# Turning 12 of 16 token tiles by DMA transposes of 16-bit planes instead of by TensorE

## The chip, the cores and the metric

The kernel runs on one core of a Trainium2 chip. The metric is the device time of one execution in microseconds, the median of several runs. The engines are called PE (TensorE, matmuls), DVE (VectorE), ACT (ScalarE), POOL (GpSimd) and SP (SyncE, which here only issues DMAs). The engines run beside one another and wait for each other by semaphores; on each engine the instructions run in a fixed order.

## The reference

The input is 2048 tokens of 512 numbers. They are normalised, and the normalised tokens go into a linear attention with a softmax feature map and into a mixture of 8 experts with two experts per token; both results are added to the input. Cut to what matters here:

```
xn = layernorm(x)                                  # x: 1 x 2048 x 512
q, k, v = split(xn @ wqkv)                         # 32 heads of 16
pq, pk = q @ w_phi, k @ w_phi                      # per head
phi(p) = concat(softmax(p), softmax(-p))
kv = phi(pk).T @ v                                 # per head, summed over all tokens
a = (phi(pq) @ kv) / (phi(pq) @ sum(phi(pk)))  @ wo
gates = softmax(xn @ wg); the two largest, scaled to sum 1
b = sum over the two of gate * (gelu(xn @ w1[e]) @ w2[e])
out = x + a + b
```

## The kernel before, in words

The 2048 tokens are 16 tiles of 128 tokens (one token per partition), and 4 chunks of 4 tiles. A tile `t` goes through these steps, each a function of the kernel:

- `load_x` loads x by DMA (two tiles share a buffer); `stats(t)` takes mean and variance on DVE; `rstds(t0, n)` makes 1/sqrt for n tiles at once: a square root on ACT and a reciprocal on DVE. `ln_stats` is stats and rstds of four tiles together. `norm(t)` normalises on DVE and stores the rows to `xn_rows` by a DMA of SP; the experts gather tokens from there later.
- `transp(t)` turns the tile, so that features lie on partitions, as a matmul's operand must: `turn` lets PE transpose four blocks of 128 x 128 into PSUM (L326); ACT then casts the result to a rounded high part `xTh` (L341), and DVE subtracts that to get the low part `xTl` (L342). Products are made of the three terms high·high, low·high and high·low, so every projection has 12 matmuls (4 blocks of features, 3 terms).
- `proj_v(t)`, `proj_k(t)` make values and key features of a tile on PE; `proj_q(c, b)` makes a quarter of the features of the queries of chunk c. ACT copies each result out of PSUM (`pV` L361, `pK` L429 and, for the gates, L430, `pQ` L479).
- The key features' softmax: `k_sub(t)` (four DVE instructions, L439 to L442), `k_exp(t)` (ACT's Exp, L449), `k_norm(t)` (three DVE instructions, L454 to L456). `kv(t)` then adds phi(k)ᵀv of the tile on PE, 64 small matmuls per tile (L501).

These steps are called one by one in an order written out by hand. The order of the calls is the order on each engine: PE, ACT, DVE and SP are queues that each run their instructions in that order, and an instruction whose input is not ready holds all behind it on its engine. PE starts with the folded weights and with tiles 0 to 3, then come the chunks of tiles 4 to 7, 8 to 11 and 12 to 15. In this stage kv of tiles 0 to 7 is made. Behind `k_norm(7)` DVE starts the routing (the first instruction is the maximum over the gates, L535), while PE goes on with the remaining queries, values and kv. After the routing come gathers and the experts.

Sqrt and Exp need different tables on ACT; a change between them loads one (the rows named ACT_TABLE_LOAD).

Buffers in SBUF are handed out from fixed pools by `slot` and given back by `free`; with `keep=True` the slot comes from the pool `keptN`.

Of the kernel before, what the change touches and what calls it, by code (L numbers as in the profile page):

```python
# [39 lines left out]
def kernel(  # L40
# [11 lines left out]
    nc = tc.nc  # L52
    P = 128
# [71 lines left out]
    def slot(shape, dt=F32, name="s", keep=False):  # L125

        n = 1
        for d in shape[1:]:
            n *= d
        words = n // 2 if dt == F16 else n  # L130
        kind = "R" if dt == F32R else "N"
        sizes = range(0 if words <= SIZES[0] else 1, 2)
        count[0] += 1
        k = choose_slot(kind, sizes, keep)
        _, b = spare[k].pop(0)
        if b is None:
# [172 lines left out]
    xn = {}  # L309

    def norm(t):
        n = slot([P, D], name="xn")
        nc.vector.tensor_scalar(n, xt[t // 2][:, t % 2, :], mv[:, t, 0:1], rstd[:, t:t + 1],
                                op0=ALU.subtract, op1=ALU.mult)
        nc.sync.dma_start(xs[t * 512:(t + 1) * 512, :].rearrange("(p a) f -> p (a f)", a=4), n)
        xn[t] = n
        if t % 2:
            free(xt.pop(t // 2))

    turned = {}  # L320

    def turn(t):
        a = bank("pT")
        turned[t] = a, bank("pT") if t < 4 else a
        for k in range(KD):
            nc.tensor.transpose(turned[t][k // 2][:, k * P:(k + 1) * P], xn[t][:, k * P:(k + 1) * P], ident)  # L326
        free(xn.pop(t))

    def transp(t):
        c, j = divmod(t, TPC)  # L330
        if j == 0:
            xTh[c] = [slot([P, 2, 512], F32R, name="xTh", keep=c == 1) for _ in range(2)]
            xTl[c] = [slot([P, 2, 512], F32R, name="xTl", keep=c == 1) for _ in range(2)]
        if t not in turned:
            turn(t)
        ps = turned.pop(t)
        for h in range(2):
            dh = xTh[c][h][:, :, j * P:(j + 1) * P]
            dl = xTl[c][h][:, :, j * P:(j + 1) * P]
            src = ps[h][:, h * 256:(h + 1) * 256].rearrange("p (k n) -> p k n", k=2)  # L340
            nc.scalar.copy(dh, src)  # L341
            nc.vector.tensor_sub(dl, src, f32(dh))  # L342
        free(*ps[:2 if t < 4 else 1])


    vt = {}
# [6 lines left out]
    def proj_v(t, then=None):  # L353
        c, j = divmod(t, TPC)
        if t % 2 == 0:
            vt[t // 2] = slot([P, 2, 32, 18], name="v", keep=t >= 8)
            nc.gpsimd.memset(vt[t // 2][:, :, :, 16:18], 1.0)
        ps = bank("pV")
        mm3(ps, [xcol(c, k, j) + (wvh[k // 2][:, k % 2, :], wvl[k // 2][:, k % 2, :]) for k in range(KD)],
            then)  # L360
        nc.scalar.copy(vt[t // 2][:, t % 2, :, 0:16], ps.rearrange("p (b j) -> p b j", j=16))  # L361
        free(ps)
        if t == NT - 1:
            free(*wvh, *wvl)
# [378 lines left out]
    def ln_stats(t0):  # L743
        for t in range(t0, t0 + TPC):
            stats(t)
        rstds(t0, TPC)
# [101 lines left out]
    proj_k(3)  # L848
    for t in range(8, 12):
        load_x(t)  # L850
    ln_stats(4)
    for t in range(4, 8):
        norm(t)
    k_sub(0)
    proj_v(0)
    proj_v(1)
    k_sub(1)
    proj_v(2)
    proj_v(3)
    for t in range(4, 8):  # L860
        transp(t)
    for t in range(8, 12):
        stats(t)
    proj_v(4)
    proj_v(5)
    rstds(8, TPC)
    for t in range(8, 12):
        norm(t)
    k_exp(0, 1)
    k_sub(2)  # L870
    proj_v(6)
    k_sub(3)
    for t in range(12, 16):
        load_x(t)
    proj_v(7)
    k_norm(0)
    proj_k(4)
    k_exp(2, 3)
    proj_k(5)
    k_norm(1)  # L880
    for t in range(8, 12):
        transp(t)
    k_norm(2)
    proj_k(6)
    k_norm(3)
    k_sub(4)
    proj_k(7)
    k_sub(5)

    for b in range(3):  # L890
        proj_q(0, b)
    kv(0)
    kv(1)
    k_exp(4, 5)
    k_norm(4)
    ln_stats(12)
    for t in range(12, 16):
        norm(t)
    k_sub(6)
    proj_k(8)  # L900
    kv(2)
    kv(3)
    proj_k(9)
    proj_k(10)
    proj_k(11)
    proj_q(0, 3)
    for t in range(12, 16):
        transp(t)
    k_norm(5)
    k_sub(7)  # L910
    k_exp(6, 7)
    k_norm(6)
    proj_k(12)
    proj_k(13)
    proj_k(14)
    kv(4)
# [796 lines left out]
```

## Time and profile before

| | |
|---|---|
| median of 3 runs | 859.4 us (858.75 to 859.9) |
| profiled execution | 858.56 us |
| its span | 856.8 us |
| granted PE clock, mean | 1.0 |
| PE busy | 851.3 us |
| DVE busy | 663.9 us |
| ACT busy | 438.7 us |
| POOL busy | 184.4 us |

The span runs from the first to the last instruction of the profiled execution; its own time is 1.76 us longer. In the rows of the timeline, the first number is the start in us from the span's start, the second the length; then come engine, line of the kernel, operation, result <- inputs with their shapes, and how many instructions the row stands for. In brackets stands the idle time of the engine just before it and what ended that. Matmuls overlap, so a row is longer than the pace at which the next one starts.

### The profile page before, as it was taken

To read this page: it belongs to the slowest core of one execution; us is meant where nothing else is said; L and a number is where in the kernel's file an instruction comes from. 1 tells how busy PE (TensorE), PEld (TensorE's weight loads), DVE (VectorE), ACT (ScalarE), POOL (GpSimd) and SP (SyncE) were. 2 spreads that over 40 slices of the span, in tenths; PEclk is the share of its full clock that TensorE was granted. 3 is DMA by queue.
4 is the path that set the end of the run, shared out by engine and by line. 5 is a ranking of instruction groups with operands and counts; after the bars stand their busy time and mean duration, and the time that the engine had idled before them with its cause. 6 is when DMAs were issued, how large, how long until landed. Compare 5 with 4: busy or idle time off the path is not lost.

```text
span 856.8 us, 15997 instructions
## 1 busy us (share of the span) xinstructions
PE 851.3 (99%) x5889; PEld 767.9 (90%) x5889; DVE 663.9 (77%) x1098; ACT 438.7 (51%) x721; POOL 184.4 (22%) x251
## 2 busy tenths in 40 slices
PE   9999999999999999999999999999999999999998
PEld 8888888899999999999999999998787888888886
DVE  6889899887783478878887877987798989846952
ACT  4453522743834364566456665465675566434541
POOL 5000002010004112511241142115511522340011
PEclk9999999999999999999999999999999999999999
DMA  8220106573317441843364346533752736539733
GB/s 298 99 99 2 50 8 191 167 231 101 123 50 221 143 133 37 253 133 113 97 200 151 111 138 159 176 110 123 229 178 87 232 115 205 175 135 384 258 115 100
DMA packets 123575, 126.99 MB, mean 148 GB/s; under 512 B 12518, under 2 KB 87782, under 8 KB 123488
## 3 DMA queue, kind: packets, MB, share of 16 engines
q1 hardware_dynamic: 115408, 106.10, 38.6%
q0 software_dynamic: 7264, 19.36, 7.0%
q8 instruction: 48, 0.79, 0.4%
q10 hardware_dynamic: 816, 0.43, 0.2%
q14 instruction: 39, 0.32, 0.1%
HBM read 98.62 MB, written 27.25 MB: 147 GB/s over the span
## 4 chain that ended last, share of the span: by engine, by line
PE 99%; DMA 0%; DVE 0%; issue 0%
PE pH L174 12%; PE pH L175 12%; PE pH L176 12%; PE pY L1296 9%; PE pY L1334 6%; PE pY L1335 6%; PE pY L1340 6%; PE pY L1266 4%; PE pY L1336 2%; PE pY L1337 2%; PE pY L1342 2%; PE pV L174 2%; PE pK L174 2%; PE pQ L474 2%; PE pV L176 2%; PE pO L176 2%
## 5 line engine op out<-in xcount | busy, mean ns | idle before, releaser
L1220 ACT ACTIVATE gl<-pH 128x276 f32<-128x276 f32 (+6 forms) x182 | 78.1, 436 | 252.6 <-PE pH L176 237.4
L1225 DVE TENSOR_TENSOR h<-gl,h 128x480 fp32r<-128x480 f32 (+6 forms) x112 | 77.8, 695 | 96.5 <-ACT h L1222 76.8
L1233 POOL DMA_INDIRECT y_rows<-keptN,pidx x83 | 90.6, 1091 | 253.3 <-ACT gl L1220 210.1
L176 PE MATMUL pH<-keptR,ws 128*128 128x258 f32 (+3 forms) x276 | 82.8, 300 | 0.0
L174 PE MATMUL pH<-keptR,ws 128*128 128x270 f32 (+3 forms) x240 | 72.5, 302 | 0.0
L175 PE MATMUL pH<-keptR,ws 128*128 128x270 f32 (+3 forms) x240 | 72.4, 301 | 0.0
L1222 ACT CAST h<-gl 128x480 fp32r<-128x480 f32 (+6 forms) x112 | 70.1, 626 | 3.6
L175 PE MATMUL pH<-xgl,ws 128*128 128x260 f32 (+3 forms) x204 | 64.6, 317 | 0.0
L174 PE MATMUL pH<-xgh,ws 128*128 128x260 f32 (+3 forms) x204 | 64.6, 317 | 0.0
L1335 PE MATMUL pY<-h,ws 128*128 128x388 f32 (+4 forms) x180 | 62.4, 347 | 0.0
L276 ACT CAST ws<-keptN 128x1024 fp32r<-128x1024 f32 x55 | 57.5, 1046 | 6.9 <-PE pY L1266 6.9
L176 PE MATMUL pH<-xgh,ws 128*128 128x272 f32 (+3 forms) x188 | 59.2, 315 | 0.0
L276 ACT CAST keptR<-keptN 128x1024 fp32r<-128x1024 f32 (+4 forms) x75 | 50.6, 705 | 16.4 <-remote 4.4
L1334 PE MATMUL pY<-h,ws 128*128 128x416 f32 (+4 forms) x168 | 58.5, 348 | 0.0
L1296 PE MATMUL pY<-h,ws 128*128 128x480 f32 x228 | 56.3, 381 | 0.0
L971 POOL DMA_INDIRECT keptN<-xn_rows,tidx x30 | 34.3, 1145 | 97.0 <-DVE vv L675 46.9
L279 DVE TENSOR_TENSOR ws<-keptN,ws 128x1024 fp32r<-128x1024 f32 x36 | 43.6, 1211 | 13.9 <-ACT ws L276 13.6
L176 PEld LDWEIGHTS pH<-keptR,ws 128*128 128x128 f32 x276 | 52.1, 189 | 1.3
L1296 PEld LDWEIGHTS pY<-h,ws 128*128 128x128 f32 x228 | 42.3, 188 | 10.8 <-issue 2.9
L175 PEld LDWEIGHTS pH<-keptR,ws 128*128 128x128 f32 x240 | 45.3, 189 | 2.2
L176 PE MATMUL pH<-xgh,keptR 128*128 128x272 f32 (+3 forms) x148 | 47.1, 318 | 0.0
L174 PEld LDWEIGHTS pH<-keptR,ws 128*128 128x128 f32 x240 | 45.1, 188 | 1.2
(339 smaller groups left out, 2397.1 us busy)
## 6 DMA issues: line engine op xcount, KB each, us to landing
keptN<-in_B_w_dram SPq DMA_DIRECT2D x172, 256.0 KB
wr<-in_B_w_dram SPq DMA_DIRECT2D x52, 256.0 KB
keptN<-y_rows SPq DMA_DIRECT2D x16, 512.0 KB
x_slots<-keptN SPq DMA_DIRECT2D x25, 256.0 KB
keptN<-in_A_x_dram SPq DMA_DIRECT2D x16, 256.0 KB
xn_rows<-keptN SPq DMA_DIRECT2D x16, 256.0 KB
keptN<-x_slots SPq DMA_DIRECT2D x32, 128.0 KB
keptN<-in_A_x_dram SPq DMA_DIRECT2D x8, 512.0 KB
```

Source lines behind the costliest of these rows:

```text
L174: nc.tensor.matmul(ps, lh, rh, start=(i == 0), stop=False)
L175: nc.tensor.matmul(ps, lh, rl, start=False, stop=False)
L176: nc.tensor.matmul(ps, ll, rh, start=False, stop=(i == n - 1))
L276: nc.scalar.copy(dst_h, src)
L1220: step[:] = [nc.scalar.activation(g[:, c:c + m], ps[:, :m], AF.Gelu_apprx_tanh)]
L1222: nc.scalar.copy(h[:, 0:full], g)
L1225: nc.vector.tensor_sub(h[:, xw:], g, f32(h[:, 0:full]))
L1233: i = nc.gpsimd.indirect_dma_start(out=to, out_offset=bass.IndirectOffsetOnAxis(ap=rows, axis=0), in_=y, in_offset=None)
L1296: nc.tensor.matmul(ps[i][:, 0:w], ws[z][:, D + i * P:D + i * P + P], h[:, low * xw:low * xw + w], start=st and k == 0, stop=last and k == ...
L1334: nc.tensor.matmul(ps[i][:, 0:w - P], vh, h[:, P:w], start=st, stop=False, skip_group_check=True)
L1335: nc.tensor.matmul(ps[i][:, 0:m], vl, h[:, P:cap], start=False, stop=False, skip_group_check=True)
L1340: nc.tensor.matmul(ps[i][:, 0:m], v[0][:, i * P:(i + 1) * P], h[:, gw + P:], start=False, stop=sp_, skip_group_check=True)
```

## The change

Tiles 4 to 15 are no longer turned by PE. A float32 number is two 16-bit numbers. For each of these tiles:

- `norm` writes the tile to the first half of a buffer of twice the size, and no longer stores it; the store is a step of its own, `keep_rows`, called later.
- `to_planes(t)`: an ACT copy of 128 x 1024 16-bit numbers (L331 of the new kernel) puts all the upper and all the lower halves of the numbers into two planes; then one DMA transpose, issued by SP (L335), turns these 8 blocks of 128 x 128 16-bit numbers into a buffer `pl`, which two tiles share.
- `to_words(t)`: an ACT copy of the same size (L340) joins the planes to float32 numbers again.
- `transp(t)` casts and subtracts as before (L365, L366), from SBUF instead of PSUM.

48 of the 64 transposes of L326 go, and with them 12 PSUM banks; 24 ACT copies and 12 DMA transposes come. `rows_apart(t)` is `keep_rows`, `to_words` and `transp`.

The order of the calls changes too. The first chunk's queries, `proj_q(0, 0)` to `proj_q(0, 3)`, stand ahead of `proj_v(4)`; before, three of them stood ahead of `kv(0)` and the last ahead of the turning of tiles 12 to 15. The loads, statistics and norms of tiles 12 to 15 come earlier; `ln_stats(12)` is taken apart into stats and `rstds(12, TPC)`. `k_norm`, `proj_k` and `k_sub` are moved among them.

```diff
     def norm(t):
-        n = slot([P, D], name="xn")
+        both = slot([P, 2, D], name="xn")
+        n = both[:, 0, :]
         nc.vector.tensor_scalar(n, xt[t // 2][:, t % 2, :], mv[:, t, 0:1], rstd[:, t:t + 1],
                                 op0=ALU.subtract, op1=ALU.mult)
-        nc.sync.dma_start(xs[t * 512:(t + 1) * 512, :].rearrange("(p a) f -> p (a f)", a=4), n)
-        xn[t] = n
+        xn[t] = both
+        if t < 4:
+            keep_rows(t)
...
+    def keep_rows(t):
+        nc.sync.dma_start(xs[t * 512:(t + 1) * 512, :].rearrange("(p a) f -> p (a f)", a=4), xn[t][:, 0, :])
+
+    def to_planes(t):
+
+        a = xn[t].bitcast(U16)
+        nc.scalar.copy(a[:, 1, :].rearrange("p (h c) -> p h c", h=2),
+                       a[:, 0, :].rearrange("p (c h) -> p h c", h=2))
+        if t % 2 == 0:
+            planes[t // 2] = slot([P, 2, D], name="pl")
+        nc.sync.dma_start_transpose(
+            planes[t // 2].bitcast(U16)[:, t % 2, :].rearrange("p (b n) -> p b n", n=P), a[:, 1, :])
+
+    def to_words(t):
+
+        nc.scalar.copy(xn[t].bitcast(U16)[:, 1, :].rearrange("p (x h) -> p h x", h=2),
+                       planes[t // 2].bitcast(U16)[:, t % 2, :].rearrange("p (h x) -> p h x", h=2))
+        if t % 2:
+            free(planes.pop(t // 2))
...
     def transp(t):
...
-        if t not in turned:
+        if t < 4 and t not in turned:
             turn(t)
-        ps = turned.pop(t)
+        ps = turned.pop(t) if t < 4 else [xn[t][:, 1, :]] * 2
...
+    def rows_apart(*ts):
+        for t in ts:
+            keep_rows(t)
+            to_words(t)
+            transp(t)
+
     ln_stats(4)
+    proj_v(0)
     for t in range(4, 8):
         norm(t)
+    to_planes(4)
+    to_planes(5)
+    proj_v(1)
     k_sub(0)
-    proj_v(0)
-    proj_v(1)
     k_sub(1)
+    to_planes(6)
+    rows_apart(4)
     proj_v(2)
+    to_planes(7)
+    rows_apart(5)
     proj_v(3)
-    for t in range(4, 8):
-        transp(t)
+    rows_apart(6)
+    proj_q(0, 0)
+    rows_apart(7)
     for t in range(8, 12):
         stats(t)
+    proj_q(0, 1)
+    proj_q(0, 2)
+    proj_q(0, 3)
     proj_v(4)
     proj_v(5)
     rstds(8, TPC)
     for t in range(8, 12):
         norm(t)
+    for t in range(12, 16):
+        load_x(t)
     k_exp(0, 1)
     k_sub(2)
     proj_v(6)
+    to_planes(8)
+    to_planes(9)
     k_sub(3)
+    proj_v(7)
+    to_planes(10)
+    to_planes(11)
     for t in range(12, 16):
-        load_x(t)
-    proj_v(7)
+        stats(t)
+    k_exp(2, 3)
+    proj_k(4)
+    rstds(12, TPC)
     k_norm(0)
-    proj_k(4)
-    k_exp(2, 3)
     proj_k(5)
+    for t in range(12, 16):
+        norm(t)
     k_norm(1)
-    for t in range(8, 12):
-        transp(t)
+    rows_apart(8, 9)
+    proj_k(6)
+    for t in range(12, 16):
+        to_planes(t)
     k_norm(2)
-    proj_k(6)
-    k_norm(3)
-    k_sub(4)
     proj_k(7)
-    k_sub(5)
-
-    for b in range(3):
-        proj_q(0, b)
+    rows_apart(10, 11)
     kv(0)
     kv(1)
+    k_norm(3)
+    proj_k(8)
+    proj_k(9)
+    k_sub(4)
+    kv(2)
+    kv(3)
+    rows_apart(12, 13)
+    proj_k(10)
+    k_sub(5)
+    rows_apart(14, 15)
+    proj_k(11)
     k_exp(4, 5)
     k_norm(4)
-    ln_stats(12)
-    for t in range(12, 16):
-        norm(t)
     k_sub(6)
-    proj_k(8)
-    kv(2)
-    kv(3)
-    proj_k(9)
-    proj_k(10)
-    proj_k(11)
-    proj_q(0, 3)
-    for t in range(12, 16):
-        transp(t)
     k_norm(5)
+    proj_k(12)
     k_sub(7)
     k_exp(6, 7)
     k_norm(6)
-    proj_k(12)
     proj_k(13)
```

On ACT, the square root of tiles 8 to 11 stood behind the casts of tiles 4 to 7 (the last two are shown) and the copies of the values of tiles 4 and 5. Before:

```order
L341 CAST keptR_95<-pT_647 128x2x128
L341 CAST keptR_96<-pT_647 128x2x128
L361 COPY keptN_88<-pV_669 128x32x16
L361 COPY keptN_88<-pV_683 128x32x16
L306 ACTIVATE rstd<-mv,epst 128x4
```

In the new kernel, from the joining copy of tile 7 on (L340), with the first queries' copies in L503 and the values' in L385:

```order
L340 COPY keptN_74<-keptN_77 128x2x512
L365 CAST keptR_95<-keptN_74 128x2x128
L365 CAST keptR_96<-keptN_74 128x2x128
L503 COPY keptN_78<-pQ_674 128x512
L503 COPY keptN_79<-pQ_688 128x512
L503 COPY keptN_79<-pQ_702 128x512
L385 COPY keptN_88<-pV_717 128x32x16
L385 COPY keptN_88<-pV_731 128x32x16
L307 ACTIVATE rstd<-mv,epst 128x4
```

Three copies of queries (the fourth stands just ahead of these rows) now lie between the last cast of tile 7 and the square root.

The square root of tiles 12 to 15 on ACT stood behind the Exps of tiles 4 and 5 and a table load. Before:

```order
L479 COPY keptN_77<-pQ_910 128x512
L449 ACTIVATE keptN_73<-keptN_73 128x1024
L449 ACTIVATE keptN_71<-keptN_71 128x1024
L306 ACT_TABLE_LOAD
L306 ACTIVATE rstd<-mv,epst 128x4
```

In the new kernel, from the copy of the values of tile 6 on (`xn_747` and the like are the buffers of tiles 8 to 11):

```order
L385 COPY keptN_87<-pV_767 128x32x16
L331 COPY xn_747<-xn_747 128x1024
L331 COPY xn_749<-xn_749 128x1024
L385 COPY keptN_87<-pV_790 128x32x16
L331 COPY xn_751<-xn_751 128x1024
L331 COPY keptN_89<-keptN_89 128x1024
L473 ACTIVATE keptN_80<-keptN_80 128x1024
L473 ACTIVATE keptN_75<-keptN_75 128x1024
L453 COPY keptN_72<-pK_822 128x32x15
L454 COPY logits<-pK_822 128x8
L307 ACT_TABLE_LOAD
L307 ACTIVATE rstd<-mv,epst 128x4
```

It now stands behind the splitting copies of tiles 8 to 11, two Exps of tiles 2 and 3 and the copy of the keys of tile 4.

On PE, one burst of 16 transposes stood between the values of tiles 3 and 4 (last matmul of one, first of the other). Before:

```order
L176 MATMUL pV_606<-keptR_93,xTl_258 128x512
L326 MATMUL pT_620<-ident,keptN_84 128x128 x4
L326 MATMUL pT_629<-ident,keptN_82 128x128 x4
L326 MATMUL pT_638<-ident,keptN_72 128x128 x4
L326 MATMUL pT_647<-ident,keptN_74 128x128 x4
L174 MATMUL pV_669<-keptR_91,keptR_95 128x512
```

In the new kernel the first queries' 48 matmuls stand in that place; their first rows behind the values of tile 3 are:

```order
L177 MATMUL pV_622<-keptR_93,xTl_258 128x512
L498 MATMUL pQ_642<-xTh_255,wfh_388 128x512
L499 MATMUL pQ_642<-xTh_255,wfl_389 128x512
L500 MATMUL pQ_642<-xTl_257,wfh_388 128x512
L498 MATMUL pQ_642<-xTh_255,wfh_388 128x512
```

The burst is gone, and four projections of queries follow the values of tile 3 ahead of the values of tile 4.

More of the change, by code (lines that the diff above doesn't have):

```diff
@@ L13 @@
 I32 = mybir.dt.int32
+U16 = mybir.dt.uint16
 AF = mybir.ActivationFunctionType
@@ L311, in norm @@
     def norm(t):
-        n = slot([P, D], name="xn")
+        both = slot([P, 2, D], name="xn")
+        n = both[:, 0, :]
         nc.vector.tensor_scalar(n, xt[t // 2][:, t % 2, :], mv[:, t, 0:1], rstd[:, t:t + 1],
                                 op0=ALU.subtract, op1=ALU.mult)
-        nc.sync.dma_start(xs[t * 512:(t + 1) * 512, :].rearrange("(p a) f -> p (a f)", a=4), n)
-        xn[t] = n
+        xn[t] = both
+        if t < 4:
+            keep_rows(t)
         if t % 2:
             free(xt.pop(t // 2))
+    def keep_rows(t):
+        nc.sync.dma_start(xs[t * 512:(t + 1) * 512, :].rearrange("(p a) f -> p (a f)", a=4), xn[t][:, 0, :])
+    planes = {}
+    def to_planes(t):
[11 more added lines that the diff above has]
+            free(planes.pop(t // 2))
     turned = {}
     def turn(t):
-        a = bank("pT")
-        turned[t] = a, bank("pT") if t < 4 else a
+        turned[t] = bank("pT"), bank("pT")
         for k in range(KD):
-            nc.tensor.transpose(turned[t][k // 2][:, k * P:(k + 1) * P], xn[t][:, k * P:(k + 1) * P], ident)
+            nc.tensor.transpose(turned[t][k // 2][:, k * P:(k + 1) * P], xn[t][:, 0, k * P:(k + 1) * P], ident)
         free(xn.pop(t))
@@ L342, in transp @@
             nc.vector.tensor_sub(dl, src, f32(dh))
-        free(*ps[:2 if t < 4 else 1])
+        free(*(ps if t < 4 else [xn.pop(t)]))
     vt = {}
@@ L355, in proj_v @@
         if t % 2 == 0:
-            vt[t // 2] = slot([P, 2, 32, 18], name="v", keep=t >= 8)
+            vt[t // 2] = slot([P, 2, 32, 18], name="v", keep=True)
             nc.gpsimd.memset(vt[t // 2][:, :, :, 16:18], 1.0)
```

## The prediction

> **What bounds the kernel now.** I read the busy table first, then PE's list of waits, then the stretches of the stage that the change touches, then the three engines row by row there. The busy table:
>
> ```profile
> span 856.8 us, 15997 instructions
> PE 851.3 (99%) x5889; PEld 767.9 (90%) x5889; DVE 663.9 (77%) x1098; ACT 438.7 (51%) x721; POOL 184.4 (22%) x251
> ```
>
> PE does matmuls for 851.3 of 856.8 us, so only PE work taken out, or PE idleness put in, can move the end. The change works between 30 and 107 us. Two stretches (columns: us, then busy us of PE, PEld, DVE, ACT, POOL; in the first DVE alone):
>
> ```profile
> 49.98:107.20 57.22, 50.91 (x83) 1.00 0.16 56
> 107.20:162.60 55.40, 55.40 (x353) 45.21 (x339) 50.08 (x178) 18.96 (x32) 5.04 (x5) 1.00 0.38 113
> ```
>
> While PE is full, DVE is at 50.9 of 57.2 us, and at 50.1 of 55.4 in the routing behind it. DVE is a second bound, with some 6 us of air before 107.20. Do the two meet? PE's rows (start, length, instruction, count):
>
> ```profile
> 40.45 1.91 PE L326 MATMUL pT<-ident,keptN 128*128 128x128 f32 x16
> 42.12 0.47 PE L174 MATMUL pV<-keptR,keptR 128*128 128x512 f32 x1
> 44.96 0.39 PE L174 MATMUL pV<-keptR,keptR 128*128 128x512 f32 x1
> 47.68 0.39 PE L174 MATMUL pV<-keptR,keptR 128*128 128x512 f32 x1
> 90.00 1.91 PE L326 MATMUL pT<-ident,keptN 128*128 128x128 f32 x16
> 99.88 1.27 PE L501 MATMUL kv<-keptN,keptN 128*18 128x32 f32 x128
> 106.69 1.46 PE L501 MATMUL kv<-keptN,keptN 128*18 128x32 f32 x128
> ```
>
> The rows of 42.12, 44.96 and 47.68 are the first matmuls of the values of tiles 4, 5 and 6: one projection of 12 matmuls takes 2.72 us. The last pair of kv (tiles 6 and 7) takes 1.46 us where the pair before took 1.27: PE waits 0.2 us in it. DVE's rows tell for what:
>
> ```profile
> 33.25 1.92 DVE L313 TENSOR_SCALAR keptN<-keptN,mv,rstd 128x512 f32<-128x512 f32 x4
> 46.33 0.68 DVE L302 BATCH_NORM_STATS2 st<-keptN 128x6 f32<-128x512 f32 x1
> 49.43 0.18 DVE L303 BATCH_NORM_AGGREGATE mv<-st 128x2 f32<-128x6 f32 x1
> 49.98 0.18 DVE L307 RECIPROCAL rstd<-rstd 128x4 f32<-128x4 f32 x1 [0.37 <-ACT rstd L306]
> 50.27 1.92 DVE L313 TENSOR_SCALAR keptN<-keptN,mv,rstd 128x512 f32<-128x512 f32 x4
> 52.10 0.68 DVE L439 TENSOR_REDUCE mk<-keptN 128x32 f32<-128x512 f32 x1
> 54.49 0.68 DVE L439 TENSOR_REDUCE mk<-keptN 128x32 f32<-128x512 f32 x1
> 63.69 0.76 DVE L342 TENSOR_TENSOR xTl<-pT,xTh 128x256 fp32r<-128x256 f32 x2 [0.44 <-ACT xTh L341]
> 67.28 0.42 DVE L342 TENSOR_TENSOR xTl<-pT,xTh 128x256 fp32r<-128x256 f32 x1 [0.44 <-ACT xTh L341]
> 67.62 1.21 DVE L454 TENSOR_REDUCE sk<-keptN 128x64 f32<-128x1024 f32 x1
> 70.59 1.21 DVE L454 TENSOR_REDUCE sk<-keptN 128x64 f32<-128x1024 f32 x1
> 84.98 0.18 DVE L307 RECIPROCAL rstd<-rstd 128x4 f32<-128x4 f32 x1 [0.36 <-ACT rstd L306]
> 91.08 0.42 DVE L342 TENSOR_TENSOR xTl<-pT,xTh 128x256 fp32r<-128x256 f32 x1 [1.59 <-ACT xTh L341]
> 95.54 0.42 DVE L342 TENSOR_TENSOR xTl<-pT,xTh 128x256 fp32r<-128x256 f32 x1 [0.44 <-ACT xTh L341]
> 107.20 0.28 DVE L535 TENSOR_REDUCE gate_max<-logits 128x16 f32<-128x128 f32 x1
> ```
>
> At 107.20 DVE has just finished k_norm(7) and starts the routing. So PE's kv(7) and DVE's k_norm(7) end together: PE has no slack against DVE there. DVE's waits between 49.98 and 107.20 are 0.36 us, 1.59 us and eight of 0.44 (the rows of 63.69 and 67.28 are first and last of four, those of 91.08 and 95.54 stand around the other four): 5.5 us in all. Per-tile prices on DVE: k_sub 2.39 us (52.10 to 54.49), k_norm 2.97 (67.62 to 70.59), four stats 3.28 (46.33 to the end of the row of 49.43), four norms 1.83 (50.27 to 52.10), one sub 0.34 (two in 0.76).
>
> **The change part by part.** *48 transposes leave PE.* The first burst of 16 holds PE from 40.45 to 42.12, 1.67 us; three such bursts are 5.0 us. This is the whole gain that the change can have.
>
> *ACT gets 24 copies of 128x1024 16-bit numbers.* No row has this form. ACT's rows of this stage, and the other prices that I need:
>
> ```profile
> 42.00 0.65 ACT L341 CAST keptR<-pT 128x256 fp32r<-128x256 f32 x2 [0.49 <-DVE keptR L342]
> 47.88 0.59 ACT L361 COPY keptN<-pV 128x512 f32<-128x512 f32 x1 [1.43 <-PE pV L176]
> 49.65 0.30 ACT L306 ACTIVATE rstd<-mv,epst 128x4 f32<-128x4 f32 x1 [1.17 <-DVE mv L303]
> 49.97 1.28 ACT L449 ACT_TABLE_LOAD   x1
> 51.26 2.01 ACT L449 ACTIVATE keptN<-keptN 128x1024 f32<-128x1024 f32 x2
> 53.17 1.06 ACT L361 COPY keptN<-pV 128x512 f32<-128x512 f32 x2
> 55.96 0.56 ACT L429 COPY keptN<-pK 128x480 f32<-128x480 f32 x1 [1.73 <-PE pK L176]
> 56.48 2.02 ACT L449 ACTIVATE keptN<-keptN 128x1024 f32<-128x1024 f32 x2
> L276 ACT CAST ws<-keptN 128x1024 fp32r<-128x1024 f32 x55 | 57.5, 1046 | 6.9 <-PE pY L1266 6.9
> q1 hardware_dynamic: 115408, 106.10, 38.6%
> 85.77 1.86 SPq L315 DMA_DIRECT2D xn_rows<-keptN  x4
> ```
>
> ACT's time goes by elements: 1024 take 1.05 us as a cast and 1.0 as an Exp. I take 0.96 us per plane copy, the pace of the two Exps from 51.26 to 53.17. Ends: 0.6 (were half the bytes to halve the time) and 1.5 (were the split into every second number slower). 24 of them are 23 us on an engine that is 51% busy. That harms only where something waits behind them.
>
> *The square root of tiles 8 to 11 is held on ACT; this decides.* Before, it stood behind the copies of pV(4) and pV(5), done at 48.5 (row of 47.88), and started at 49.65 when the statistics were ready. Now the copies of all four first queries and of pV(4) and pV(5) stand ahead of it, and each waits for PE. PE is in order: from the end of pV(3) at 40.45 come six projections, 6 x 2.72 = 16.3, ending at 56.8. The copy of pV(5) starts 0.2 later, as in the row of 47.88 (pV(5) ended on PE at 47.68). 0.5 later ACT is free: square root at 57.5, reciprocal on DVE at 57.85 instead of 49.98. DVE has done everything that stands ahead of the reciprocal, the same work as before, by about 50 to 51. So it idles some 7 us, and all behind comes 7.9 later.
>
> *The square root of tiles 12 to 15* follows on ACT behind: the root of tiles 8 to 11 and a table load (1.6 us), two Exps (1.91), copy pV(6) 0.5, two planes 1.91, copy pV(7) 0.5, two planes 1.91, two Exps 1.91, copies of pK(4) and its logits 0.52 (55.96 to 56.48), a table load 1.28, the root 0.3. That is 12.3 from 57.5: ready at 69.9. DVE, from 57.85, has 0.29 + 1.83 for the norms, 4.78 for two k_sub and 3.28 for the stats, and is there at 68.0: a new wait of 1.9. From 69.9 follow k_norm(0), the norms of tiles 12 to 15 and k_norm(1), 7.8 us: k_norm(1) ends at 77.7. PE is at kv(1) at 73.5 (56.8 + two values 5.4, four keys at 2.64, an estimate of 496/512 of 2.72, and kv(0) 0.64). It waits 4.2 us: the gain is used up there.
>
> *Up to k_norm(4).* DVE: four subs 1.36, k_norm(2), four subs, k_norm(3): 8.7, to 86.4; PE's kv(3) waits about 2 more. PE then does kv(3) and pK(10), whose copy starts at 86.4 + 0.64 + 2.64 + 0.2 = 89.9. ACT behind it: that copy and logits 0.52, two joining copies 1.91, four casts 1.2 with 0.2 of waits among them, pK(11) 0.52, table load 1.28, Exp 1.06: 96.6. DVE has two k_sub and eight subs in that time, 7.5, to 93.9, and waits 2.7 for the Exp. From 96.6 four k_norm and two k_sub, 16.7: routing starts at 113.3 instead of 107.20, 6.1 later. DVE's work is the same; its old 5.5 us of waits fall away (it comes later, and the casts no longer alternate with it behind a burst of PE), 1.9 + 2.7 come.
>
> *The end.* kv(7) on PE follows k_norm(7), and PE's instructions behind it are those of before (PE 55.40 of 55.40 busy), so the end shifts by the same 6.1 us. As PE's sum: 5.0 out, about 11 of waits at kv(1), kv(3), kv(5) and kv(7) in.
>
> *The 12 DMA transposes on SP, and the moved stores and loads.* The trace has no transpose. Lower end: as an ordinary transfer of 256 KB, four of which are issued in 1.86 us, 0.5 us each. From the queue row, 38.6% of 16 engines and 856.8 us over 115408 packets is 46 ns per packet on one engine. Rows of 128 16-bit numbers (256 bytes) would make 1024 packets, 2.9 us on 16 engines; rows of 16 numbers (32 bytes) 8192 packets, 23.5 us, the upper end. I take 2.9, the form that the change writes. Cover: the planes of tiles 4 to 7 start about 35 (norms from 33.25, one plane copy), and DVE must have their last sub by 54.2 to end the next stats by 57.5; with 2.0 for joining, casts and sub, four serial transposes have 35 to 52.2, 4.3 us each. So 2.9 costs nothing; were the held root gone, DVE would wait for these instead. The 12 stores, 0.47 each on SP, and the loads of tiles 12 to 15 stand between them; their readers (stats at 64.7, the gathers after the routing) come much later.
>
> Sum: 858.56 (the profiled execution) + 6.1 = 864.7. The median of the runs is 859.4, 0.84 above the profiled one: 865.5. A difference of 0.2% (1.7 us) is about what a measurement of this kernel can tell.
>
> **The rivals.**
>
> *A: the cover holds, the gain arrives.* If DVE were not late at kv(7), PE would keep its 5.0 us: 854.4. DVE would have to make up 7.9 us with 5.5 of old waits and no new one. The point that decides is the held root: every us it comes before 57.5 is one less, and gain begins only below about 52. PE's 2.72 us per projection speaks against it.
>
> *B: only the held root costs.* ACT's other queues hide (plane copies at 0.6 us): 7.9 - 5.5 = 2.4 later, 861.8.
>
> *C: slow transposes.* Above 4.3 us each, every us costs four at tiles 4 to 7 and something again in the two later groups: at 5 us 2.8 there and, serial from the planes at 62 and at 75, about 1 and 4: 873; at 10 us over 900. The page "VectorE: DVE Perf Modes" of the Trainium skill (section "The three transpose paths" and the rules behind it) speaks for it: it gives 1309 ns for a 128x128 of 16 bits by DMA against 390 on TensorE, and advises TensorE where the result may go to PSUM. An estimate from that page: eight such blocks per tile, 10.5 us if they go one after another. No trace here shows the DMA's price yet; PE's own, 1.67 us for 16, is far under 390 ns each.
>
> *D: slower split and join.* At 1.5 us per copy, 0.54 more on six copies ahead of the two late roots and Exps is 3.3, and about as much again ahead of the subs: 869 to 872.
>
> *E: a cold PE.* These rows are the same eight matmuls, early and later:
>
> ```profile
> 3.79 1.94 PE L378 MATMUL pF<-ident,keptN 128*128 128x128 f32 x8 [0.19 <-DMA keptN<-in_A_wqkv_dram]
> 8.62 1.04 PE L378 MATMUL pF<-ident,keptN 128*128 128x128 f32 x8
> ```
>
> PE starts at half pace. If a wait of 4.2 us brings that back, the projection behind it takes 2.7 us longer; at kv(3) and kv(7) PE has 2 us of waiting to pay it from, so the sum grows by 1 to 2: 867. The page "TensorE: Matmul & The Clock Gate" (its rules) warns of idle gaps above about 3 us; no run here shows one mid-kernel.
>
> **How the numbers follow.** Forecast: 0.48, 863 to 868. E: 0.12. D: 0.12. C: 0.13. B: 0.08. A: 0.04. No change within 1.7 us, should DVE's work shrink as well: 0.03. The range of 862 to 877 leaves out A, the no-change case, half of B and most of C. Slower 0.93, same 0.03, faster 0.04.
>
> **What would show it.** Right: the wait of DVE's reciprocal at about 57.8 is near 7 us, released by ACT's root, whose own wait ends with PE's pV(5); PE's list of waits names kv <- DVE with two of about 4 us; PE busy falls by 5 us while the span grows; routing starts near 113. Wrong: the joining copies wait long for DMA (C), or kv shows no waits (A).

## The result and the profile after

| | before | after |
|---|---|---|
| median | 859.08 us (4 runs) | 868.69 us (4 runs, 867.61 to 869.88) |
| ratio, 95% interval | | 1.0113 [1.0095, 1.0130] |
| profiled execution, its span | 858.56, 856.8 us | 869.88, 868.0 us |
| granted PE clock, mean | 1.0 | 0.992 |

The changed kernel is 9.6 us slower, against 6.1 forecast; 868.69 us lies in the range (862 to 877) and 3.2 above the number (865.5), just outside the 863 to 868 that had the chance of 0.48. In the series of runs behind the ratios further below, five executions took 1039 us or more and are left out of the ratios. The head of the page after, and PE's list of waits (engine and line that waits, what it waits for; us in all, times, longest):

```profile
span 868.0 us, 15947 instructions
PE 850.8 (98%) x5841; PEld 766.4 (88%) x5841; DVE 663.1 (76%) x1098; ACT 465.3 (54%) x745; POOL 183.5 (21%) x251
PE kv L525 <- DVE keptN L480: 9.2, 4, 4.6
```

PE has 48 instructions less, but is busy for only 0.5 us less, and waits 9.2 us for DVE at kv, where before it waited some 0.2. DVE's rows at the places of the forecast, from the timeline after:

```profile
33.95 1.91 DVE L315 TENSOR_SCALAR keptN<-keptN,mv,rstd 128x512 f32<-128x512 f32 x4
58.49 0.18 DVE L308 RECIPROCAL rstd<-rstd 128x4 f32<-128x4 f32 x1 [5.77 <-ACT rstd L307]
70.58 0.18 DVE L308 RECIPROCAL rstd<-rstd 128x4 f32<-128x4 f32 x1 [1.98 <-ACT rstd L307]
98.66 1.22 DVE L478 TENSOR_REDUCE sk<-keptN 128x64 f32<-128x1024 f32 x1 [2.45 <-ACT keptN L473]
115.36 0.28 DVE L559 TENSOR_REDUCE gate_max<-logits 128x16 f32<-128x128 f32 x1
```

The reciprocals of tiles 8 to 11 and of tiles 12 to 15 and `k_norm(4)` each wait for ACT, and the routing starts at 115.36 instead of 107.20. (The norms of tiles 4 to 7 already start 0.7 later than before, 33.95 against 33.25. This start moves by about as much from profile to profile: the reciprocal ahead of the norms stood between 32.17 and 33.73 in the first eight kernels of this study. So 0.7 is not put down to the change.) PE's rows, and then PE alone in two stretches (us, PE busy and instructions, granted clock, DMA share, GB/s):

```profile
78.66 0.80 PE L525 MATMUL kv<-keptN,keptN 128*18 128x32 f32 x64 [4.08 <-DVE keptN L480]
79.96 0.61 PE L176 MATMUL pK<-wfl,xTh 128*128 128x496 f32 x1
80.38 0.61 PE L177 MATMUL pK<-wfh,xTl 128*128 128x496 f32 x1
82.73 0.39 PE L177 MATMUL pK<-wfh,xTl 128*128 128x496 f32 x1
87.44 0.73 PE L525 MATMUL kv<-keptN,keptN 128*18 128x32 f32 x64 [0.30 <-DVE keptN L480]
107.24 1.06 PE L525 MATMUL kv<-keptN,keptN 128*18 128x32 f32 x64 [4.64 <-DVE keptN L480]
```

```profile
80.00:82.00 2.00, 2.00 (x6) 0.50 1.12 92
108.00:112.00 4.00, 4.00 (x32) 0.50 0.02 4
```

After the two waits of 4.08 and 4.64 us PE runs at clock 0.50: a key matmul then comes every 0.41 us (0.42 from the row of 79.96 to that of 80.38) instead of 0.22. It happens to 7 key matmuls and part of an eighth at the first place and to 12 at the second; with the slower kv that is some 4.2 us, taken from the starts of the rows. So PE's account is 5.0 out, 9.0 of waits in, 4.2 of half pace in, and the start of 0.7: 8.9 of the 9.36 us by which PE's last matmul ends later (861.99 against 852.63). The rest, some 0.5, I could not place. That PE seems as busy as before is those slow matmuls.

On ACT and SP the new steps look like this (SPq are SP's DMA issues):

```profile
34.53 2.00 ACT L331 COPY keptN<-keptN 128x1024 uint16<-128x1024 uint16 x2 [0.35 <-DVE keptN L315]
35.60 4.07 SPq L335 DMA_TRANSPOSE keptN<-keptN  x3
38.53 1.36 ACT L340 COPY keptN<-keptN 128x1024 uint16<-128x1024 uint16 x1 [0.58 <-DMA keptN<-keptN]
57.67 0.59 ACT L385 COPY keptN<-pV 128x512 f32<-128x512 f32 x1 [2.13 <-PE pV L177]
58.16 0.30 ACT L307 ACTIVATE rstd<-mv,epst 128x4 f32<-128x4 f32 x1
q1 hardware_dynamic: 128080, 109.24, 39.8%
```

A splitting copy (L331) goes at about 0.96 us, a joining copy (L340) takes 1.36. From the first issue of a transpose to the joining copy that it releases are 2.9 us. The square root of tiles 8 to 11 stands right behind the copy of pV(5), which PE released. A window over all engines (busy us of PE, PEld, DVE, ACT, POOL) shows what ACT does from there to 77 us:

```profile
57.70:77.00 19.30, 16.66 (x136) 13.77 (x134) 16.25 (x31) 19.18 (x29) 0.21 (x1) 1.00 0.32 82
```

ACT, 54% busy over the span, is busy 19.18 of 19.30 us here, while PE (16.66) and DVE (16.25) both have waits.

### The profile page after: what moved, and what is told of

The parts are those of the page before. It is cut to its first block, busy times and chain, and to the rows that moved or that the text cites. A ratio compares the mean times of both kernels' runs of the same rounds, so it can differ in the third digit from the quotient of the medians.

```text
span 868.0 us, 15947 instructions
## 1 busy us (share of the span) xinstructions
PE 850.8 (98%) x5841; PEld 766.4 (88%) x5841; DVE 663.1 (76%) x1098; ACT 465.3 (54%) x745; POOL 183.5 (21%) x251
## 4 chain that ended last, share of the span: by engine, by line
PE 93%; ACT 3%; DVE 2%; DMA 1%; issue 0%; SPq 0%
PE pH L175 12%; PE pH L176 12%; PE pH L177 12%; PE pY L1340 9%; PE pY L1378 6%; PE pY L1379 6%; PE pY L1384 6%; PE pY L1310 4%; PE pY L1381 2%; PE pY L1380 2%; PE pY L1386 2%; PE pQ L498 2%; PE pO L177 2%; PE pO L176 2%; PE pQ L499 2%; PE pQ L500 2%
## 5 line engine op out<-in xcount | busy, mean ns | idle before, releaser
L1269 DVE TENSOR_TENSOR h<-gl,h 128x480 fp32r<-128x480 f32 (+6 forms) x112 | 77.8, 694 | 96.6 <-ACT h L1266 69.6
```

Source lines behind the costliest of these rows:

```text
L1269: nc.vector.tensor_sub(h[:, xw:], g, f32(h[:, 0:full]))
```

## The experiments

Each ratio is to the kernel before on the same chip, with its 95% interval. The diffs, cut at `...`, are against the changed kernel where nothing else is said.

**The held square root alone.** The root of tiles 8 to 11 is called as soon as its statistics are there.

```diff
     for t in range(8, 12):
         stats(t)
+    rstds(8, TPC)
     proj_q(0, 1)
...
     proj_v(5)
-    rstds(8, TPC)
```

> The changed kernel with one call moved: rstds(8) stands right behind the statistics of tiles 8 to 11, ahead of proj_q(0,1). Theory 1 (the prediction's: the held square root is the price): the root no longer waits for the copies of pQ and pV(5); DVE's reciprocal comes at about 53 us instead of 58.5, everything behind it 5 us earlier, 863 to 864 us. Theory 2 (the root was only the first of a queue on ACT): the Exps of tiles 0 and 1 and the splitting copies still start behind pV(5)'s copy at 57.7, so the square root of tiles 12 to 15 still comes at about 70.2; DVE's wait of 5.8 us vanishes at the first reciprocal and the wait of 2.0 at the next one grows to about 7.5; the time stays at 868 to 869 us.

868.82 us (865.29 to 870.13), ratio 1.0125 [1.0107, 1.0143]: nothing gained. The profiled execution was the shortest of the four, 865.29 us; its reciprocal ahead of the norms of tiles 4 to 7 came 1.46 us earlier than that of the changed kernel. The two reciprocals on DVE:

```profile
51.62 0.18 DVE L308 RECIPROCAL rstd<-rstd 128x4 f32<-128x4 f32 x1 [0.36 <-ACT rstd L307]
68.94 0.18 DVE L308 RECIPROCAL rstd<-rstd 128x4 f32<-128x4 f32 x1 [7.19 <-ACT rstd L307]
```

The first wait is gone; the second has grown from 1.98 to 7.19. What stands ahead of the second root on ACT (Exps, value copies, splitting copies) still starts behind the copy of pV(5). So the held root is where the lateness was seen, not what it cost: ACT's queue behind it is as late without it.

**Both roots and the Exps of tiles 0 and 1 freed.** The root of tiles 8 to 11 stands behind its statistics; Exps 0 and 1 and the norms of tiles 8 to 11 behind the third query; the splits of tiles 8 to 11 and the statistics of tiles 12 to 15 stand ahead of `proj_v(6)`, the root of tiles 12 to 15 ahead of `proj_v(7)` and Exps 2 and 3.

```diff
+    rstds(8, TPC)
     proj_q(0, 1)
     proj_q(0, 2)
+    k_exp(0)
+    k_exp(1)
+    norm(8)
...
     proj_q(0, 3)
...
     k_sub(2)
-    proj_v(6)
+    k_sub(3)
     to_planes(8)
...
+    proj_v(6)
+    rstds(12, TPC)
+    proj_v(7)
+    k_exp(2)
+    k_exp(3)
     proj_k(4)
-    rstds(12, TPC)
     k_norm(0)
```

> As e1, and the second root is freed too: the Exps of tiles 0 and 1 stand behind the copies of pQ(0,1) and pQ(0,2), the key subtractions of tiles 2 and 3 and the splitting copies of tiles 8 to 11 behind pV(5), the statistics and the square root of tiles 12 to 15 ahead of pV(7) and of the Exps of tiles 2 and 3. Theory 1: with both roots early DVE has no wait above 1.5 us left, about 861 to 862 us. Theory 2 (ACT as a whole is too full in 50 to 97 us, with 24 copies of 1.0 and 1.36 us): the wait moves on, to the casts of tiles 8 to 11 that stand behind the joining copies (3 us at the first sub) and to those of tiles 12 to 15; 1 us is gained, about 867.5 us.

865.58 us (865.05 to 866.16), ratio 1.0083 [1.0065, 1.0102]. About 3 us come back, and PE still waits 8.1 us at kv (after: 9.2). DVE:

```profile
63.70 0.18 DVE L308 RECIPROCAL rstd<-rstd 128x4 f32<-128x4 f32 x1 [1.50 <-ACT rstd L307]
79.07 0.76 DVE L366 TENSOR_TENSOR xTl<-keptN,xTh 128x256 fp32r<-128x256 f32 x2 [3.10 <-ACT xTh L365]
DVE xTl L366 <- ACT xTh L365: 6.9, 5, 3.1
```

The second root came 6.9 us earlier than in the changed kernel (1.0 of it from the start of the stage), and the wait turned up at the next thing that ACT makes, the casts of tiles 8 to 15 (6.9 us in five waits; 1.2 in two in the changed kernel). The gain, 3.2 us against the run before on the same chip, was about three times the 1 us that I had expected; the kind, a wait that moves along ACT's queue, was right.

**Keeping PE busy in its two long waits.** Small matmuls of zeros, which nothing uses, stand ahead of `kv(1)` and `kv(5)`.

```diff
     kv(0)
+    warm = bank("warm")
+    idling(28, 256)
+    free(warm)
     kv(1)
...
     kv(4)
+    warm = bank("warm")
+    idling(32, 256)
+    free(warm)
     kv(5)
```

> The changed kernel with idle matmuls (28 and 32 of 128x128 by 256 in 16 bits, about 0.11 us each at full pace) ahead of kv(1) and kv(5), where PE waits 4.1 and 4.6 us. They add work that nothing needs. Theory 1 (a wait of 4 us puts PE to half pace): with about 1 us of idle time left, the granted clock stays at 1.0, the keys behind kv(1) and kv(5) run at 0.22 us per matmul instead of 0.41, PE is at kv(6) before DVE is done with k_norm(7), and the end comes 1.0 to 1.5 us earlier, about 867.4 us. Theory 2 (the slow pace there has another cause, as the DMA traffic at 78 to 88 us): the keys stay at 0.41 us and the time does not fall.

867.25 us (865.55 to 868.46), ratio 1.0097 [1.0076, 1.0118]; that interval overlaps the changed kernel's, so it is the profile that decides:

```profile
73.54 3.23 PE L774 MATMUL warm<-idle 128*128 128x256 f16 x28
77.69 0.72 PE L525 MATMUL kv<-keptN,keptN 128*18 128x32 f32 x64 [0.92 <-DVE keptN L480]
78.67 0.39 PE L176 MATMUL pK<-wfl,xTh 128*128 128x496 f32 x1
78.90 0.39 PE L177 MATMUL pK<-wfh,xTl 128*128 128x496 f32 x1
108.00:114.00 6.00, 5.27 (x85) 4.09 (x83) 5.86 (x7) 2.63 (x7) 0.00 (x0) 1.00 0.01 3
```

The keys behind the filled wait come every 0.23 us and the clock stays at 1.00. The DMA engines are busy there too (share 0.85 from 80 to 84 us, with the clock at 1.00), so it is not their traffic that halves the pace. The end of kv(7) lies 7.12 us behind that of before instead of 9.36; less the start of this profile, which was 0.97 earlier than that of the changed kernel, that is 1.3 us for the half pace. The rule of the Trainium skill in "TensorE: Matmul & The Clock Gate" (section "Why this matters for your kernels", "No PE-idle gaps >~3µs") agrees with the waits of 4.08 and 4.64 us; further below, the fifth and the seventh experiment show half pace behind somewhat shorter ones.

**The splitting copies on POOL.**

```diff
-        nc.scalar.copy(a[:, 1, :].rearrange("p (h c) -> p h c", h=2),
+        nc.gpsimd.tensor_copy(a[:, 1, :].rearrange("p (h c) -> p h c", h=2),
                        a[:, 0, :].rearrange("p (c h) -> p h c", h=2))
```

> The changed kernel with the 12 splitting copies on POOL instead of ACT, all else in the same order. ACT loses 12 copies of 0.96 us. Theory 1 (held roots alone): the root of tiles 8 to 11 still waits for pV(5), and DVE's wait there stays; but behind it ACT reaches the root of tiles 12 to 15 four copies earlier, so about 2 us are gained (DVE's work then fills the time), 866 to 867 us. Theory 2 (ACT's fill decides): the casts come earlier too, 865 to 867 us. If POOL needs more than about 3 us per copy, the joining copies wait for the transposes instead and nothing is gained.

870.02 us (868.85 to 871.07), ratio 1.0130 [1.0111, 1.0148]: no better, though ACT has 11 us less to do. The timeline of DVE and POOL shows a price elsewhere:

```profile
33.41 3.36 DVE L315 TENSOR_SCALAR keptN<-keptN,mv,rstd 128x512 f32<-128x512 f32 x4
34.02 4.62 POOL L331 COPY keptN<-keptN 128x1024 uint16<-128x1024 uint16 x4 [13.24 <-DVE keptN L315]
37.28 0.68 DVE L464 TENSOR_REDUCE mk<-keptN 128x32 f32<-128x512 f32 x1
37.88 1.31 DVE L465 TENSOR_TENSOR keptN<-keptN,mk 128x512 f32<-128x512 f32 x1
```

While POOL copies, the four norms on DVE take 3.36 us instead of 1.91 and a subtraction 1.31 instead of 0.68; the reductions stay at 0.68. The section "Who interferes with whom" of the page "SBUF — State Buffer" of the Trainium skill says that the norms' kind of operation and operations with two inputs in SBUF can contend with POOL for a port pair that DVE and POOL share, and that reductions on this chip never do. The trace agrees, with 3.36, 1.31 and 0.68 us. DVE's busy time grew by 5.7 us, and PE still waits 11.4 us at kv (5.9 put down to DVE, 5.5 to ACT).

**The new order without the DMA transposes.** PE turns all tiles again; the calls stay in the new order, and those of `to_planes` and `to_words` return at once.

```diff
+    BY_DMA = ()
...
     def to_planes(t):
+        if t not in BY_DMA:
+            return
...
     def to_words(t):
+        if t not in BY_DMA:
+            return
...
-        if t < 4 and t not in turned:
+        if t not in BY_DMA and t not in turned:
             turn(t)
```

> The new order of calls, but tiles 4 to 15 are turned by PE again, each where its joined planes were cast: no 16-bit planes, no DMA transposes, 48 transposes back on PE. Theory 1 (the order's held roots are the price, and the turning by DMA is not): PE has 5 us more to do, the root of tiles 8 to 11 still stands behind the queries and pV(5), DVE waits 9 to 10 us for it, and the kernel is slower than the changed one, 870 to 873 us. Theory 2 (the 24 ACT copies are the price): ACT loses 28 us of work, DVE's waits shrink, and the time falls to 863 us or less.

870.06 us (869.0 to 872.89), ratio 1.0144 [1.0118, 1.0171]. The row of the first reciprocal:

```profile
58.84 0.18 DVE L308 RECIPROCAL rstd<-rstd 128x4 f32<-128x4 f32 x1 [9.47 <-ACT rstd L307]
```

The order alone costs as much as the whole change, without one plane copy on ACT. PE waits here too, in its rows and in a stretch behind the second wait (us, PE busy and instructions, granted clock, DMA share, GB/s):

```profile
88.04 1.06 PE L531 MATMUL kv<-keptN,keptN 128*18 128x32 f32 x64 [3.77 <-DVE keptN L486]
110.01 0.89 PE L531 MATMUL kv<-keptN,keptN 128*18 128x32 f32 x64 [2.94 <-DVE keptN L486]
112.00:114.00 2.00, 2.00 (x7) 0.56 0.00 0
```

So a wait of 2.94 us, a little under the "~3" of that rule, already brings half pace.

**The old order with the DMA transposes.** The calls stand as in the kernel before; the splits stand behind each norm, store and join in front of each cast.

```diff
     k_norm(1)
-    rows_apart(8, 9)
+    rows_apart(8)
+    rows_apart(9)
+    rows_apart(10)
+    rows_apart(11)
+    k_norm(2)
     proj_k(6)
-    for t in range(12, 16):
-        to_planes(t)
-    k_norm(2)
```

> The old order of calls with the new way of turning: the splitting copies and transposes stand right behind the norms of each chunk, store, joining copy, casts and subs where the tiles were turned on PE; proj_q stays where it was. Theory 1 (held roots alone): both roots are early again, DVE loses little, PE is 5 us shorter: 854 to 858 us. Theory 2 (the way norm, split, transpose, join, cast, sub is some 9 to 13 us long and has to be covered on PE): PE waits 2 to 3 us at proj_v(4) and 8 to 10 us at proj_k(12), the second of these waits brings the half pace, and the time is 868 to 873 us; the new order then was needed for the new way.

870.13 us (869.13 to 871.65), ratio 1.0140 [1.0119, 1.0161]. PE's list and the matmul that it names first:

```profile
PE pK L175 <- ACT xTh L365: 8.5, 1, 8.5
PE pV L175 <- ACT keptR L365: 2.3, 1, 2.3
99.97 0.78 PE L175 MATMUL pK<-wfh,xTh 128*128 128x496 f32 x1 [8.55 <-ACT xTh L365]
```

PE now waits for the turned tiles themselves, since in the old order they are needed soon after their norms. So the change needed another order than that of before, and the new one that it came with lost what the transposes freed.

**Each transpose issued twice,** one run.

```diff
-        nc.sync.dma_start_transpose(
+        for _ in range(2):
+         nc.sync.dma_start_transpose(
```

> The changed kernel with each DMA transpose issued twice, to the same place (12 more transposes that nothing needs). One takes SP 1.25 to 1.5 us to issue. Theory 1 (they are hidden behind the held roots): the first reciprocal stays at about 58, and the time changes by less than 2 us. Theory 2 (SP and the DMA engines have no room): the joining copies of tiles 4 to 7 wait up to 1.5 us each, those of tiles 12 to 15 wait for transposes and stores that end 6 us later, and the time grows by 5 to 9 us.

876.08 us (one run, no interval), 7.4 above the median of the changed kernel on another chip. SP's issues, the worst of DVE's rows, and PE's last wait at kv:

```profile
34.11 12.66 SPq L336 DMA_TRANSPOSE keptN<-keptN  x6
103.60 1.10 DVE L367 TENSOR_TENSOR xTl<-keptN,xTh 128x256 fp32r<-128x256 f32 x3 [11.43 <-issue]
116.92 1.00 PE L526 MATMUL kv<-keptN,keptN 128*18 128x32 f32 x64 [2.84 <-DVE keptN L481]
```

An issue takes 2.1 us here against 1.36, so SP pays more than twice the price; why is not shown (the second transpose writes to the same place as the first and may wait for it). All the run shows is that there is no room for transposes at such a price; it does not say that one costs 7.4/12 us. PE's wait of 2.84 us is followed by clock 0.50 again (from 119 to 120 us).

**Another order, same work.** ACT's queue is arranged so that roots, Exps and splits stand ahead of copies that wait for PE; the calls on the other engines move with it. The stretch with the first queries, of some 130 calls that are moved:

```diff
+    rstds(8, TPC)
     proj_v(3)
...
+    transp(7)
     proj_q(0, 2)
-    proj_q(0, 3)
+    k_exp(0)
     proj_v(4)
     proj_v(5)
-    rstds(8, TPC)
...
+    norm(8)
...
+    k_exp(1)
...
+    to_planes(8)
+    stats(14)
+    stats(13)
+    proj_q(0, 3)
+    norm(9)
+    norm(10)
+    to_planes(10)
+    stats(15)
     k_sub(2)
+    rstds(12, TPC)
```

> The turning by DMA of the changed kernel, unchanged, with the calls between ln_stats(4) and k_norm(7) in another order, chosen so that no instruction on ACT stands behind a copy that waits longer for PE than it need: the first root behind the queries' second copy, the second root ahead of the Exps of tiles 2 and 3, each joining copy well ahead of its cast, and kv with a key projection or two between them, so that PE has no wait of over 2 us. Theory A (the 9.6 us are a matter of the order alone, and the 5 us of PE can be had): DVE loses about 5 us in waits from 49 us on as before, PE keeps its clock, routing starts 2 to 3 us earlier than in the kernel before, 856 to 857 us. Theory B (24 copies on ACT and the chain over the DMA are too long whatever the order): DVE waits for casts again, 860 us or more.

856.66 us (855.57 to 857.35, 11 runs), ratio 0.9979 [0.9970, 0.9988]: 0.2% faster than the kernel before, with an interval that stays below 1, and well below the ratio of the changed kernel. DVE's only wait above 0.4 us between the subtractions of tiles 4 to 7 and the routing, the start of the routing, PE's list, and a window over all engines:

```profile
59.43 0.18 DVE L308 RECIPROCAL rstd<-rstd 128x4 f32<-128x4 f32 x1 [1.61 <-ACT rstd L307]
103.14 0.28 DVE L565 TENSOR_REDUCE gate_max<-logits 128x16 f32<-128x128 f32 x1
PE kv L531 <- DVE keptN L486: 0.8, 1, 0.8
60.00:80.00 20.00, 19.17 (x268) 15.53 (x267) 19.72 (x31) 19.99 (x33) 0.99 (x5) 1.00 0.53 133
```

ACT is as full as in the changed kernel (19.99 of 20.00 us), but DVE now works 19.72 of the 20. The second root comes at 59.4 instead of 70.6, and the routing starts 4.06 us earlier than before. PE's last matmul ends 4.05 earlier. Of that 1.9 us reach the span and 1.4 the median, as the stretch behind the last matmul is 6.3 us here against 4.2 before.

**That order with PE turning.** The planes and their copies do nothing in it: no tile is on the list of those turned by DMA. The diff is against the run before.

```diff
-    BY_DMA = (4, 5, 6, 7, 8, 9, 10, 11, 12, 13, 14, 15)
+    BY_DMA = ()
```

> The order of calls of the run before this one, but PE turns the tiles again (no planes, no DMA transposes). Theory A (with the order right the DMA way is worth its 5 us of PE): PE is 5 us longer and DVE's subs again wait for casts behind PE's transposes: 5 to 6 us slower than the run before, 861 to 863 us. Theory B (the gain of the run before, if it has one, comes from the better order, and the way of turning gives nothing): the same time or less.

860.94 us (860.8 to 861.46, 7 runs), ratio 1.0031 [1.0019, 1.0042]. Against 856.66 on the same chip, the DMA transposes are worth 4.3 us in an order that can use them; PE freed 5.0. In the two profiles PE's last matmul is 6.9 us apart (848.58 and 855.43); the stretch behind it, 6.3 against 3.9, takes part of that back.

**The long stretch at the end.** If the 12 transposes shifted the turn in which DMAs take their completion semaphores, four more stores (those of tiles 12 to 15, halved and so doubled in number) might shift it back, as 12 and 4 are two turns of eight. The first edit is on the reordered kernel, the second the same on the changed one, the third repeats the first.

```diff
-        nc.sync.dma_start(xs[t * 512:(t + 1) * 512, :].rearrange("(p a) f -> p (a f)", a=4), xn[t][:, 0, :])
+        dst = xs[t * 512:(t + 1) * 512, :].rearrange("(p a) f -> p (a f)", a=4)
+        for h in ((slice(0, 64), slice(64, P)) if t >= 12 else (slice(0, P),)):
+            nc.sync.dma_start(dst[h], xn[t][h, 0, :])
```

> The kernel of e8 with the four row stores of tiles 12 to 15 issued in two halves of 64 partitions each: four more DMAs, same bytes. In e8 the last matmul comes 4.1 us earlier than before, but the median only 1.4 us: 6.3 us lie between the last matmul and the end, 4.2 before. The DMAs take eight completion semaphores in turn, and the 12 transposes shift the turn by four, so that ACT's last stores now wait first for the load that lands last. Theory A (the shifted turn): 16 more DMAs are two full turns, ACT waits for each load in the order of landing as before, the tail shrinks to 4 to 4.5 us, 854.5 to 855.5 us. Theory B (the tail is longer for another reason, such as the scatters landing later): it stays at 5.5 to 6.3 us, 856.5 us.

> The changed kernel with the same split of the stores of tiles 12 to 15. Theory A: the tail behind the last matmul, 6.0 us in its profile, shrinks to 4 to 4.5 us, and the time falls by 1 to 2 us to about 867.3 us; the difference is what the shifted turn of semaphores adds to the loss. Theory B: no change, 868.7 us.

> The kernel of e10 once more, because in the runs of e10 the kernel before itself spread over 6.5 us, which hides an effect of 1 to 2 us. Theory A (the shifted turn of the completion semaphores makes the tail longer): ratio to the kernel before about 0.9955 to 0.9965, tail behind the last matmul 4 to 4.6 us in the profile. Theory B: ratio 0.998 as in e8, tail 5.5 us or more.

The first two ran on a chip on which the kernel before itself spread from 857.75 to 864.3 us, and their times settle nothing: 859.19, ratio 0.9979 [0.9961, 0.9997], and 870.2, ratio 1.0119 [1.0087, 1.0151]. Their profiles have 6.4 and 4.4 us behind the last matmul. The third, on another chip, where the kernel before lay between 857.62 and 859.04 us, gave 856.57 us (854.91 to 857.69, 11 runs), ratio 0.9978 [0.9968, 0.9987], with 6.3 us behind the last matmul as without the edit. So the stores gain nothing on the reordered kernel. The 4.4 us of the changed kernel with the edit, against 6.0 without, would fit the shifted turn; but the first three experiments, with as many DMAs as the changed kernel and no edit of the stores, have 4.4, 4.9 and 4.6 us. The shifted turn alone therefore does not make the stretch long. In the reordered kernel the last addition waits for a load, where before it waited for PE:

```profile
848.75 0.42 DVE L1614 TENSOR_TENSOR gl<-gl,pO 128x256 f32<-128x256 f32 x1 [1.15 <-DMA gl<-out_dram]
```

In the third run of the split stores it waits for PE again, and the stretch is as long. What makes it 3.8 to 6.4 us long from profile to profile (before 4.2, after 6.0) stays open.

Put together, as ratios to the kernel before on the same chip:

| | PE turns | DMA turns |
|---|---|---|
| order of before | 1 | 1.0140 [1.0119, 1.0161] |
| order of the change | 1.0144 [1.0118, 1.0171] | 1.0113 [1.0095, 1.0130] |
| the third order | 1.0031 [1.0019, 1.0042] | 0.9979 [0.9970, 0.9988] |

## Why the prediction was right, and where it was off

- *Sign and mechanism.* That PE's gain is used up at kv by a DVE chain held by ACT was right. The forecast had two waits of about 4 us at kv; they are 4.08 and 4.64. But in all it had about 11 us of waits there and no half pace in the sum; it became 9.2 of waits and some 4.2 of half pace, so that the number came as near as it did is in part luck.
- *The root of tiles 8 to 11.* Forecast 57.85; measured 58.49, of which 0.7 is the later start. DVE idled 5.77 us instead of 7, as it had already waited 5.9 us in the subtractions of tiles 4 to 7. The forecast had no wait there; on ACT each of these tiles takes about 2.48 us (a join, two casts, a copy of PE's results), and DVE's subtractions wait for it.
- *"This decides".* This step failed as a cause. Under rival A the prediction said that every us by which the held root comes before 57.5 "is one less". The root called earlier, and done 6.9 us earlier (1.5 of it from the start of the stage), gained nothing (the wait of 7.19 us in the first experiment). What decides is the order of the calls as a whole: the table above tells it apart from the way of turning. That ACT's queue is the part of it that matters is what the waits show; the third order moved the calls of the other engines as well.
- *The root of tiles 12 to 15* was forecast at 69.9 with a wait of 1.9 and came at 70.58 with 1.98; without the 0.7 that is exact. kv(3) waited 0.30 instead of 2, because PE came late itself, at half pace.
- *The Exp ahead of k_norm(4): the mis-sized term.* I had 96.6, it was 98.66, 1.36 late beside the start. The joining copy took 1.36 us, not 0.96. ACT's rows from the last copy that waited for PE, the copy of pK(10), the joining copy of tile 15, and the Exp, and PE's first matmul behind pK(10):

```profile
86.51 0.56 ACT L453 COPY keptN<-pK 128x480 f32<-128x480 f32 x1 [2.06 <-PE pK L177]
91.08 0.56 ACT L453 COPY keptN<-pK 128x480 f32<-128x480 f32 x1
93.63 1.36 ACT L340 COPY keptN<-keptN 128x1024 uint16<-128x1024 uint16 x1
97.57 2.01 ACT L473 ACTIVATE keptN<-keptN 128x1024 f32<-128x1024 f32 x2
90.89 0.39 PE L175 MATMUL pK<-wfh,xTh 128*128 128x496 f32 x1
```

  ACT does not wait between the first and the last of its rows, and four joining copies lie there, 4 x 0.40 = 1.6 us over their price. Only two of them are sure to count: PE was done with pK(10) at about 90.89, so its copy could not have started before about 91.08 however short the two joins ahead of it. That start is 0.5 behind the forecast (89.9 and the 0.7), as k_norm(3) and kv(3) came later; the joins of tiles 14 and 15 add 0.8. The splitting copy was priced right. Rival D had this size, 1.36 of its 1.5, but for half of the copies only.
- *Half pace (rival E, 0.12)* happened, at both long waits. At the first it was nearly free, as forecast, since PE had slack at kv(3). At the second it added about 1.2 us at the end. I had taken half pace to be the unlikely case because no run had shown a wait of that length in mid-kernel; the rows of the cold start (1.94 against 1.04 for the same eight matmuls) deserved more than 0.12.
- *The sum.* From span to span: 6.1 forecast, 0.7 start, 1.4 at the Exp (0.8 of it two joining copies), 1.2 half pace, 1.8 behind the last matmul (6.0 against 4.2): 11.2, which is 868.0 less 856.8. The last term was in no rival, and its cause is open. The medians differ by 9.6 only, as the profiled execution, 869.88 us, was the slowest of the four.
- *The DMA transposes (rival C).* 2.9 us taken, 2.9 measured, and hidden as forecast but for 0.58 us that ACT waited at the first join. The packets grew by 12,674 over all queues, 1056 for each transpose, which bears out the 1024 of the forecast. That the time agrees is in part luck: the forecast priced the packets alone, while the measured 2.9 us begin with some 1.36 us of issuing. The estimate of 10.5 us per tile from "VectorE: DVE Perf Modes" (section "The three transpose paths") of the Trainium skill was not borne out: eight blocks in one transfer took 2.9 us here, far from eight times 1309 ns.
- *What was to show it:* PE busy was to fall by 5 and fell by 0.5, as half pace counts as busy; where the clock stays up it falls by 4.8 (846.5 in the third order with DMA turning).

## What to carry to other kernels

On an engine that runs its queue in order, a small step that others wait for (a root, an Exp, a cast), placed behind copies that wait for PE, inherits PE's time; moving that one step only hands the wait to the next in the queue, so the queue is better ordered as a whole, and judged by the waits of the engine behind it. Work taken off the bounding engine pays only if the second bound's chain is shortened or at least kept: here, beside PE turning in the same order, the same transposes cost 1.4% in the order of before and gained 0.5% in the third. When forecasting a wait of some 3 us or more on PE, add the half pace behind it.

## What the hardware showed that I had not expected

- PE's clock fell to 0.50 at or behind every wait of 2.84 us or more in these traces (2.84 with each transpose issued twice, 2.94 and 3.77 in the new order with PE turning, 4.08 and 4.64 after, 8.55 in the old order with DMA turning), for some 3 to 6 us of work; behind 2.33 us (old order, DMA turning) it did not.
- The clock does not fall at a fixed time after PE goes idle. In the changed kernel PE is idle from 74.58 to 78.66 us, and the clock is 1.00 up to 78 us, 0.79 in the mean from 78 to 80, and 0.50 from 80 on. With the splits on POOL, PE is idle from 74.49 us, and the clock is 0.50 from 76 us on already.
- An ACT copy of 128x1024 16-bit numbers takes 1.36 us when it writes every second number (joining) and about 0.96 when it reads every second (splitting).
- Beside a POOL copy in SBUF, four of DVE's norms took 3.36 us instead of 1.91 and a subtraction 1.31 instead of 0.68; the reductions beside it stayed at 0.68.
- A DMA transpose of 128x1024 16-bit numbers within SBUF took 1.25 to 1.5 us to issue on SP, and 2.9 us from the start of the first one's issue to the copy that it released.
